# Two of a weight's four column means computed behind the first attention, a new order of the first loads, lone columns by VectorE, last stores by SP

## The chip, the cores and the metric

The kernel runs on one core of one Trainium2 chip. The metric is the device time of one execution in microseconds (us). PE in the profile is TensorE, PEld its weight loads, DVE is VectorE, ACT is ScalarE, POOL is GpSimd, SP is SyncE. "Granted clock" is the share of its full clock that TensorE was given: 1.00 is full, 0.50 is half.

Only one core runs, so there is no second die to compare with. Every ratio below compares runs of two kernels on one chip, interleaved in the same rounds; e9, e12 and e8 before ran on another chip than the other eight experiments.

## The reference

A hash attention (a query sees only the keys whose six sign bits equal its own), then a Fourier mix, a layer norm and a two-layer network:

```python
# q, k, v: (4, 8, 768, 64) f32; proj (64, 6); w_ch1 (512, 2048); w_ch2 (2048, 512)
q_bucket = np.sum((q @ proj > 0) * powers, axis=-1)      # k_bucket the same
scores = np.where(q_bucket == k_bucket, q @ k.T / 8, -1e9)
attn = softmax(scores) @ v                               # sum + 1e-9 below
x = attn as (B, S, H*D) = (4, 768, 512)
u = x + real(fft(fft(x, axis=1), axis=2))
un = (u - mean(u)) / sqrt(var(u) + 1e-6)
out = u + np.maximum(un @ w_ch1, 0) @ w_ch2
```

## The kernel before

The batch is walked in four attentions, each of four head pairs of six key blocks; the mix of one batch is woven between the attention steps of the next. In the first attention there is no mix yet, and there the weight `w1` is prepared: it is turned into the number form that the matmuls use ("narrowing"), and the mean of each column is taken off it, so that the layer norm needs no subtraction. The mean is a matmul with a constant tile. In the kernel before, each of the four column groups of 512 has its mean taken at once when its four slices are narrowed:

```python
def weights(wsb, wdr):
    ...                                   # (cut: buffers, fetches)
    for i, (dst, src) in enumerate(slices):
        if wide:
            narrow(dst, ...)              # 3 VectorE, 3 ScalarE instructions
        fetch(i + depth, nc.gpsimd)
        yield
        if wsb is w1 and i % NDC == NDC - 1:
            f = i // NDC * WC
            ps = pt([P, WC], f"wm{f}")    # a PSUM buffer from a shared pool
            for c in range(NDC):          # NDC = 4
                nc.tensor.matmul(ps, mean, w1[:, c, f : f + WC],
                                 start=(c == 0), stop=(c == NDC - 1))
            for c in range(NDC):
                w = w1[:, c, f : f + WC]
                nc.vector.tensor_tensor(w, w, ps, op=ALU.subtract)
```

The transposes of q and k (`trq`, `trk`) go through the same PSUM pool and are emptied into `qt` and `kt` by VectorE or ScalarE. `fold`, the first part of the mix, has most of its work on VectorE and a small copy of two lone columns on ScalarE, and is started in the last head pair of an attention:

```python
# in attention(b), for each key block c
if c > 1:
    next(half, None)                      # one step of fold(b, 0), last head pair only
...
# in fold
nc.scalar.copy(z[:, :, 2 * n + 1 : 2 * n + 3], f[:, :, 0 : n + 2 : n + 1])
```

The first loads, the bit weights `pw` and the stores follow. The first bits matmuls read `qt` and `pjw`, not `pw`; but the cast of `pw` stands in VectorE's order among the copies that empty `qt`, so they wait for it all the same:

```python
def load(n, others=nc.sync):
    for nm, src in (("q", q), ("k", k), ("v", v)):
        for h in range(2):
            (nc.sync if nm == "q" else others).dma_start(...)
load(0, nc.scalar)                        # q by SP, k and v by ScalarE's queue
...                                       # (cut: proj, off)
nc.sync.dma_start(pwf, cn["pw"].ap())
nc.vector.tensor_copy(pw, pwf)
...
def store(b, T, src):
    nc.gpsimd.dma_start(out[b, ...], src[...])
```

At the very end stands a conditional: a slower general version of the kernel for inputs with very large scores or weights of an unexpected form. With these inputs it is never taken, but every engine has to branch over it.

Of the kernel before, what the change touches and what calls it, by code (L numbers as in the profile page):

```python
# [10 lines left out]
F32 = mybir.dt.float32  # L11
# [5 lines left out]
ALU = mybir.AluOpType  # L17
# [461 lines left out]
def _main(  # L479
# [33 lines left out]
    def pt(shape, name):  # L513

        turn[0] += 1
        if roomy[0] and turn[0] % 2:
            if turn[0] % 4 == 1:
                return ps_o.tile(shape, F32, tag="o", name=name)
            return ps_sc.tile(shape, F32, tag="sc", name=name)
        return ps_1.tile(shape, F32, tag="ps", name=name)  # L520
# [11 lines left out]

    nat = {}

    def load(n, others=nc.sync):
        b, t = divmod(n, NPAIR)
        for nm, src in (("q", q), ("k", k), ("v", v)):
            tag, bufs = ("vn", 2) if nm == "v" else ("qkn", 2)
            tl = wt([P, NT, 2, D], F32, tag, f"{nm}n{n}", bufs)
            for h in range(2):  # L540
                (nc.sync if nm == "q" else others).dma_start(
                    tl[:, :, h, :], src[b, 2 * t + h].rearrange("(p c) d -> p c d", c=NT)
                )
            nat[nm, n] = tl

    warm = const.tile([1, 1], F32, tag="warm", name="warm")
    nc.gpsimd.memset(warm, 0.0)
    load(0, nc.scalar)
    nc.scalar.activation(warm, warm, AF.Exp)

    ident = const.tile([P, P], F32, tag="ident", name="ident")
# [7 lines left out]
        nc.sync.dma_start(pjw[h * D : (h + 1) * D, h * D : h * D + NBITS], proj)  # L559
    off = const.tile([P, 2], F32, tag="off", name="off")  # L560
    nc.sync.dma_start(off, cn["off"].ap())
    pj = const.tile([P, 32], F32, tag="pj", name="pj")
    nc.gpsimd.memset(pj, 0.0)
    for h in range(2):
# [31 lines left out]
    def narrow(dst, raw, low, col):  # L596
# [20 lines left out]
            t, t, AF.Relu, bias=least, scale=-1.0, accum_out=strange[:, col : col + 1]  # L617
        )

    def weights(wsb, wdr):  # L620

        wide = wdr.dtype == I64
        slices = [
            (wsb[:, c, f : f + WC], wdr[c * P : (c + 1) * P, f : f + WC])
            for f in range(0, wdr.shape[1], WC)
            for c in range(wdr.shape[0] // P)
        ]
        raws, masks = [], []
        if wide:
            zt = wt([P, 3, 2 * WC], F32, "z", f"zraw{wdr.shape[0]}", 1)  # L630
            raws += [zt[:, i] for i in range(3)]
            if wsb is w1:
                ft = wt([P, 12, WC], F32, "F", "fraw", 1)
                raws += [
                    ft[:, i : i + 2].rearrange("p i w -> p (i w)") for i in range(0, 8, 2)
                ]
                masks = [ft[:, i] for i in range(8, 12)]

        def fetch(i, queue):
            if i < len(slices):  # L640
                dst, src = slices[i]
                if wide:
                    raw = raws[i % len(raws)].bitcast(I32)
                    queue.dma_start(raw.bitcast(I64), src)
                else:
                    queue.dma_start(dst, src)

        depth = len(raws) or 4
        for i in range(depth):
            fetch(i, nc.sync if wsb is w1 else nc.gpsimd)  # L650
            if wsb is w1 and i == 1:
                load(1)
# [3 lines that stand above are left out]
                mask = masks[i % 4] if masks else wt([P, WC], F32, "u", f"mask{i}", 2)  # L656
                narrow(
                    dst, raws[i % len(raws)].bitcast(I32), mask.bitcast(I32),
                    i if wsb is w1 else len(slices) + i,
                )  # L660
            fetch(i + depth, nc.gpsimd)
            yield
            if wsb is w1 and i % NDC == NDC - 1:

                f = i // NDC * WC
                ps = pt([P, WC], f"wm{f}")
                for c in range(NDC):
                    nc.tensor.matmul(  # L668
                        ps, mean, w1[:, c, f : f + WC],
                        start=(c == 0), stop=(c == NDC - 1),  # L670
                    )
                for c in range(NDC):
                    w = w1[:, c, f : f + WC]
                    nc.vector.tensor_tensor(w, w, ps, op=ALU.subtract)


    xs = {}
# [167 lines left out]
    def attention(b):  # L845
        xs[b] = wt([P, NPAIR, S], F32, "x", f"x{b}")
        pending = []

        def finish():
            n, c, pk, oos, accs = pending.pop(0)  # L850
            values(n, c, pk, oos)
            if c == NT - 1:
                scale(n, oos, accs)

        for t in range(NPAIR):
            n = NPAIR * b + t
            half = fold(b, 0) if t == NPAIR - 1 else iter(())
            if 1 < n + 1 < NPAIR * B:
                load(n + 1)
            ahead = prepare(n + 1) if n + 1 < NPAIR * B else iter(())  # L860
            oos = [ps_o.tile([P, 512], F32, tag="o", name=f"oo{n}_{g}") for g in range(2)]
            accs = [wt([P, 2, HALF], F32, "t3", f"acc{n}_{g}", 4) for g in range(2)]
            first = None
            for c in range(NT):
                new = [weigh(n, g, c) for g in range(2)]
                if c == 0:
                    first = new
                else:
                    for g in range(2):
                        nc.vector.tensor_tensor(  # L870
                            accs[g], first[g][:, :, 0:HALF] if c == 1 else accs[g],
                            new[g][:, :, 0:HALF], op=ALU.add,
                        )
                while pending:
                    finish()
                pending.append((n, c, new, oos, accs))
                if c > 1:
                    next(half, None)
                if c > 0:
                    next(ahead, None)  # L880
                yield
        while pending:
            finish()
# [5 lines left out]
    def store(b, T, src):  # L889

        blk, r = divmod(T * P, HALF)
        at = 0
        while at < P:
            par, i = divmod(r + at, HW)
            w = min(P - at, HW - i)
            s0 = blk * HALF + 2 * i + par
            nc.gpsimd.dma_start(  # L897
                out[b, s0 : s0 + 2 * w - 1 : 2, :], src[at : at + w]
            )
            at += w  # L900
# [8 lines left out]
    def fold(b, cp):  # L909



        x = xs[b]
        if cp == 0:
            zs[b] = wt([P, 2, 2, 2, HALF], F32, "z", f"z{b}", 1)
        for pc in range(2):
            e = wt([P, S], F32, "t3", f"e{b}_{cp}_{pc}", 4)
            nc.vector.tensor_tensor(
                e, x[:, cp], x[:, cp + 2], op=ALU.subtract if pc else ALU.add
            )  # L920
            f = wt([P, 2, HALF], F32, "t3", f"f{b}_{cp}_{pc}", 4)
            for par in range(2):
                nc.vector.tensor_tensor(
                    f[:, par], e[:, 0:HALF], e[:, HALF:S],
                    op=ALU.subtract if par else ALU.add,
                )
            z = zs[b][:, cp, pc]
            n = HALF // 4 - 1
            for at, op in ((0, ALU.add), (2 * n + 3, ALU.subtract)):

                for i, first, last in ((0, 1, n), (n, 2 * n + 2, n + 1)):
                    nc.vector.tensor_tensor(
                        z[:, :, at + i : at + i + last], f[:, :, first : first + last],
                        turned(f, 2 * n + 1 if i == 0 else HALF - 1, last), op=op,
                    )
            nc.scalar.copy(
                z[:, :, 2 * n + 1 : 2 * n + 3], f[:, :, 0 : n + 2 : n + 1]
            )
            yield
# [136 lines left out]
    with tc.manual_schedule(engines={ET.PE, ET.DVE, ET.Activation, ET.Pool}):  # L1076
        for _ in prepare(0):
            pass
        roomy[0] = False
        for i, _ in enumerate(attention(0)):  # L1080
            if i % 5 < 4:
                next(other, None)
        for _ in other:
            pass
    for b in range(B):
        if b > 0:



            wait = 0  # L1090
            if b == 1:
                next(other)
                next(other)
                wait = 2
            steps, done = NPAIR * NT - wait, 2 if b == 1 else 0
            for i, _ in enumerate(attention(b), 1):
                while done * steps < (MIX - LEFT) * (i - wait):
                    next(other)
                    done += 1
# [73 lines left out]
```

## Time and profile before

| what | value |
|---|---|
| time | 1232.55 us median of 6 runs (1231.4 to 1234.67) beside the changed kernel; 1232.8 when the prediction was made |
| TensorE busy | 1187.7 of the 1231.7 us span |
| first matmul / first scores | 7.15 / 14.40 us |
| scale of the first attention's last head pair (VectorE's copy `vs`) | 144.28 us |
| first `trk` transposes behind it | 159.19 us |
| last matmul's end, and from there to the end of the span | 1223.79 us, 7.94 us |

In these tables "scale" is VectorE's copy `vs`, its first step of the division that ends a head pair. The hand-over is the stretch from there to the `trk` transposes of the next attention; `h` is the first layer of the network.

The page's rows by fortieths of the span (30.8 us each; a digit is the busy share in tenths, PEclk the granted clock in tenths) show in one look where there is room:

```profile
PE   7987989999999999999999999999999999999997
DVE  4888759853365547645357464754435653311110
PEclk9999989999999999999999999999999999999999
```

TensorE is short of nine tenths in the first slice, in three slices between 61 and 185 us and in the last. The dip of the clock row to 8 is the slice from 154 to 185 us, behind the wait of 3.53 us before `trk`. VectorE is at seven or eight tenths from 31 to 154 us, where `w1` is prepared.

### The profile page before, as it was taken

The numbers are of one execution on the slowest core, as the hardware profiler recorded it, in microseconds if no ns is written. First come the engines' busy times: TensorE is split into PE (matmuls) and PEld (weight loads), VectorE is DVE, ScalarE is ACT, GpSimd is POOL, SyncE is SP. The second block draws the span as 40 slices with busy tenths as digits, with TensorE's granted clock in tenths as the row PEclk, the third lists the DMA queues.
The fourth block names the chain that finished last, engine by engine and source line by source line (L and its number), as shares of the span: only waits on it lengthen the run. The fifth ranks groups of instructions, "written<-read, shape, count | busy, mean of one in ns | idle before, by whom it ended". The sixth has DMA issues, their size and how long they took to land.

```text
span 1231.7 us, 11839 instructions
## 1 busy us (share of the span) xinstructions
PE 1187.7 (96%) x4585; PEld 592.8 (48%) x4585; DVE 633.8 (51%) x1186; ACT 348.1 (28%) x625; POOL 57.3 (5%) x127
## 2 busy tenths in 40 slices
PE   7987989999999999999999999999999999999997
PEld 4433455444454446444444445544445445754553
DVE  4888759853365547645357464754435653311110
ACT  6876337731222113221223213122112211000000
POOL 1000001101100010000000010000000000001000
PEclk9999989999999999999999999999999999999999
DMA  9421214401010010100101011010000000000000
GB/s 290 127 71 27 47 42 136 153 14 35 18 26 14 22 28 15 24 16 13 43 9 39 1 30 35 1 39 1 22 9 9 1 10 18 1 1 17 9 9 19
DMA packets 82880, 44.24 MB, mean 36 GB/s; under 512 B 76800, under 2 KB 76928, under 8 KB 82816
## 3 DMA queue, kind: packets, MB, share of 16 engines
q1 hardware_dynamic: 74032, 23.22, 7.7%
q0 software_dynamic: 5648, 19.40, 5.0%
q10 hardware_dynamic: 3136, 0.79, 0.4%
q8 instruction: 38, 0.62, 0.2%
q14 instruction: 26, 0.21, 0.1%
HBM read 37.10 MB, written 6.29 MB: 35 GB/s over the span
## 4 chain that ended last, share of the span: by engine, by line
PE 78%; DVE 13%; ACT 4%; issue 2%; DMA 2%; POOL 0%; SPq 0%; POOLq 0%; DVEq 0%; ACTq 0%
PE h L1012 26%; PE o L1040 25%; PE sc L790 9%; PE oo L810 7%; DVE acc L870 3%; DVE pk L799 3%; PE cs L958 2%; ACT pk L796 2%; PE B L987 2%; PE wm L668 1%; PE A L987 1%; PE sum L827 1%; DMA zraw<-in_moe_w_ch_dram 1%; DVE w L607 1%; DVE w L612 1%
## 5 line engine op out<-in xcount | busy, mean ns | idle before, releaser
L1012 PE MATMUL h<-x,w 128*128 128x384 f32 x1024 | 343.5, 491 | 4.8 <-ACT qt L530 2.4
L1040 PE MATMUL o<-w,h 128*128 128x512 f32 x768 | 339.8, 596 | 0.0
L1012 PEld LDWEIGHTS h<-x,w 128*128 128x128 f32 x1024 | 191.0, 190 | 149.3 <-issue 10.4
L799 DVE SCALAR_TENSOR_TENSOR pk<-qb,kb,pk 128x384 f32<-128x384 bf16 x264 | 151.3, 615 | 184.2 <-ACT pk L796 184.0
L1040 PEld LDWEIGHTS o<-w,h 128*128 128x128 f32 x768 | 142.5, 190 | 174.8 <-issue 167.2
L796 ACT ACTIVATE pk<-sc 128x768 f32<-128x768 f32 x192 | 148.8, 809 | 231.3 <-PE sc L790 193.5
L790 PE MATMUL sc<-qt,kt 64*128 64x384 f32 x768 | 191.2, 511 | 0.0
L810 PE MATMUL oo<-pk,vn 128*64 128x385 f32 (+1 forms) x768 | 145.2, 499 | 0.0
L870 DVE TENSOR_TENSOR acc<-acc,pk 128x768 f32<-128x768 f32 x128 | 120.2, 955 | 9.1 <-ACT pk L796 7.5
L790 PEld LDWEIGHTS sc<-qt,kt 64*128 64x128 f32 x768 | 78.4, 188 | 67.4 <-issue 44.3
L1021 ACT ACTIVATE h<-h 128x384 f32<-128x384 f32 x64 | 31.3, 489 | 272.1 <-PE h L1012 272.0
L1019 DVE TENSOR_SCALAR h<-h 128x384 f32<-128x384 f32 x64 | 35.4, 554 | 141.2 <-PE h L1012 141.2
L1046 DVE SCALAR_TENSOR_TENSOR u<-o,rs,u 128x512 f32<-128x512 f32 x24 | 18.0, 751 | 166.7 <-PE o L1040 106.5
L810 PEld LDWEIGHTS oo<-pk,vn 128*64 128x64 f32 x768 | 46.5, 136 | 87.8 <-issue 82.1
L1030 ACT COPY u<-un 128x512 f32<-128x512 f32 x24 | 13.9, 585 | 111.5 <-PE un L1028 111.5
L1036 POOL TENSOR_SCALAR rs<-mv 128x1 f32<-128x1 f32 x24 | 7.7, 321 | 595.5 <-DVE mv L1034 590.6
L897 POOL DMA_DIRECT2D out_dram<-u x32 | 19.4, 607 | 317.1 <-DVE u L1046 255.5
L958 PE MATMUL cs<-ch,z 128*128 128x128 f32 (+3 forms) x192 | 32.1, 321 | 1.2 <-ACT qt L530 1.2
L958 PEld LDWEIGHTS cs<-ch,z 128*128 128x128 f32 x192 | 28.4, 197 | 9.1 <-issue 2.8
L870 DVE TENSOR_TENSOR acc<-pk,pk 128x768 f32<-128x768 f32 x32 | 30.0, 951 | 2.0 <-ACT pk L796 1.7
L965 ACT COPY F<-cs 128x257 f32<-128x257 f32 (+1 forms) x32 | 11.1, 374 | 67.7 <-PE cs L958 67.7
L987 PE MATMUL B<-sq,F 128*128 128x193 f32 (+1 forms) x128 | 26.3, 332 | 1.5 <-DVE bt L747 1.3
(105 smaller groups left out, 799.3 us busy)
## 6 DMA issues: line engine op xcount, KB each, us to landing
zraw<-in_moe_w_ch_dram POOLq DMA_DIRECT2D x21, 512.0 KB, 4.2
qn<-in_q_dram SPq DMA_DIRECT2D x32, 192.0 KB, 3.2
vn<-in_v_dram SPq DMA_DIRECT2D x30, 192.0 KB, 3.2
kn<-in_k_dram SPq DMA_DIRECT2D x30, 192.0 KB, 3.2
out_dram<-u POOLq DMA_DIRECT2D x16, 256.0 KB, 2.4
fraw<-in_moe_w_ch_dram SPq DMA_DIRECT2D x4, 512.0 KB, 7.5
fraw<-in_moe_w_ch_dram POOLq DMA_DIRECT2D x4, 512.0 KB, 4.3
out_dram<-u POOLq DMA_DIRECT2D x16, 128.0 KB, 2.4
```

Source lines behind the costliest of these rows:

```text
L790: nc.tensor.matmul(ps[:, h, 0:HALF], kt[rows, ks], qt[rows, qs], start=kb is not None, stop=True,)
L796: nc.scalar.activation(pk[:, :, 0:HALF], ps[:, :, 0:HALF], AF.Exp, scale=SCALE)
L799: nc.vector.scalar_tensor_tensor(pk[:, h, 0:HALF], qb[:, h, qs], kb[:, h, c : c + 1], pk[:, h, 0:HALF], op0=ALU.is_equal, op1=ALU.mult,)
L810: nc.tensor.matmul(oos[g][h * D : (h + 1) * D, 0:w], nat["v", n][:, c, h, :], pk[g][:, h, 0:w], start=(c == 0), stop=(c == NT - 1),)
L870: nc.vector.tensor_tensor(accs[g], first[g][:, :, 0:HALF] if c == 1 else accs[g], new[g][:, :, 0:HALF], op=ALU.add,)
L897: nc.gpsimd.dma_start(out[b, s0 : s0 + 2 * w - 1 : 2, :], src[at : at + w])
L958: nc.tensor.matmul(ps[:, pc + 2 * lo : pc + 2 * hi - 1 : 2], z[:, cp, pc, par, t * P : (t + 1) * P], ch[:, cp, pc, lo:hi], start=(cp == 0) ...
L987: nc.tensor.matmul(ps[:, cols], F[:, par, k, t, j * P : (j + 1) * P], sq[:, t, k, cols], start=(t == 0), stop=(t == 1),)
L1012: nc.tensor.matmul(ps, w1[:, c, fc * P : (fc + 1) * P], x[:, c, g * HALF : (g + 1) * HALF], start=(c == 0), stop=(c == NDC - 1),)
L1019: nc.vector.tensor_scalar(hr, ps, 0.0, None, op0=ALU.max)
L1021: nc.scalar.activation(hr, ps, AF.Relu)
L1040: nc.tensor.matmul(ps, hs[fc][:, j * P : (j + 1) * P], w2[:, fc, :], start=(fc == 0), stop=(fc == NFC - 1),)
```

## The change

The intent: the third and the fourth mean leave the first attention and are taken together right behind it, kept in two SBUF tiles by ScalarE and subtracted in the hand-over to the second attention. `fold` starts a key block later and its lone columns go to VectorE, so that ScalarE no longer stands behind VectorE's fold. The first loads are asked for in the order q, k, then v: of q and k a half on each of two queues, v on SP's alone. The last batch's stores go by SP instead of GpSimd, so that GpSimd can finish early. The whole diff:

```diff
--- before.py
+++ after.py
@@ -532,20 +532,21 @@
 
     nat = {}
 
-    def load(n, others=nc.sync):
+    def load(n, names="qkv", second=nc.sync):
         b, t = divmod(n, NPAIR)
-        for nm, src in (("q", q), ("k", k), ("v", v)):
+        for nm in names:
+            src = {"q": q, "k": k, "v": v}[nm]
             tag, bufs = ("vn", 2) if nm == "v" else ("qkn", 2)
             tl = wt([P, NT, 2, D], F32, tag, f"{nm}n{n}", bufs)
             for h in range(2):
-                (nc.sync if nm == "q" else others).dma_start(
+                (second if h else nc.sync).dma_start(
                     tl[:, :, h, :], src[b, 2 * t + h].rearrange("(p c) d -> p c d", c=NT)
                 )
             nat[nm, n] = tl
 
+    load(0, "qk", nc.scalar)
     warm = const.tile([1, 1], F32, tag="warm", name="warm")
     nc.gpsimd.memset(warm, 0.0)
-    load(0, nc.scalar)
     nc.scalar.activation(warm, warm, AF.Exp)
 
     ident = const.tile([P, P], F32, tag="ident", name="ident")
@@ -559,6 +560,7 @@
         nc.sync.dma_start(pjw[h * D : (h + 1) * D, h * D : h * D + NBITS], proj)
     off = const.tile([P, 2], F32, tag="off", name="off")
     nc.sync.dma_start(off, cn["off"].ap())
+    load(0, "v")
     pj = const.tile([P, 32], F32, tag="pj", name="pj")
     nc.gpsimd.memset(pj, 0.0)
     for h in range(2):
@@ -616,6 +618,19 @@
         nc.scalar.activation(
             t, t, AF.Relu, bias=least, scale=-1.0, accum_out=strange[:, col : col + 1]
         )
+
+    def average(f):
+        ps = pt([P, WC], f"wm{f}")
+        for c in range(NDC):
+            nc.tensor.matmul(
+                ps, mean, w1[:, c, f : f + WC], start=(c == 0), stop=(c == NDC - 1)
+            )
+        return ps
+
+    def centre(f, avg):
+        for c in range(NDC):
+            w = w1[:, c, f : f + WC]
+            nc.vector.tensor_tensor(w, w, avg, op=ALU.subtract)
 
     def weights(wsb, wdr):
 
@@ -662,16 +677,10 @@
             yield
             if wsb is w1 and i % NDC == NDC - 1:
 
+
                 f = i // NDC * WC
-                ps = pt([P, WC], f"wm{f}")
-                for c in range(NDC):
-                    nc.tensor.matmul(
-                        ps, mean, w1[:, c, f : f + WC],
-                        start=(c == 0), stop=(c == NDC - 1),
-                    )
-                for c in range(NDC):
-                    w = w1[:, c, f : f + WC]
-                    nc.vector.tensor_tensor(w, w, ps, op=ALU.subtract)
+                if f < DFF // 2:
+                    centre(f, average(f))
 
 
     xs = {}
@@ -874,7 +883,7 @@
                 while pending:
                     finish()
                 pending.append((n, c, new, oos, accs))
-                if c > 1:
+                if c > 2:
                     next(half, None)
                 if c > 0:
                     next(ahead, None)
@@ -894,7 +903,7 @@
             par, i = divmod(r + at, HW)
             w = min(P - at, HW - i)
             s0 = blk * HALF + 2 * i + par
-            nc.gpsimd.dma_start(
+            (nc.sync if b == B - 1 else nc.gpsimd).dma_start(
                 out[b, s0 : s0 + 2 * w - 1 : 2, :], src[at : at + w]
             )
             at += w
@@ -933,7 +942,7 @@
                         z[:, :, at + i : at + i + last], f[:, :, first : first + last],
                         turned(f, 2 * n + 1 if i == 0 else HALF - 1, last), op=op,
                     )
-            nc.scalar.copy(
+            nc.vector.tensor_copy(
                 z[:, :, 2 * n + 1 : 2 * n + 3], f[:, :, 0 : n + 2 : n + 1]
             )
             yield
@@ -1082,6 +1091,10 @@
                 next(other, None)
         for _ in other:
             pass
+        means = []
+        for f in range(DFF // 2, DFF, WC):
+            means.append((f, wt([P, WC], F32, "u", f"mean{f}", 2)))
+            nc.scalar.copy(means[-1][1], average(f))
     for b in range(B):
         if b > 0:
 
@@ -1091,6 +1104,8 @@
             if b == 1:
                 next(other)
                 next(other)
+                for f, avg in means:
+                    centre(f, avg)
                 wait = 2
             steps, done = NPAIR * NT - wait, 2 if b == 1 else 0
             for i, _ in enumerate(attention(b), 1):
```

## The prediction

> **What bounds the kernel now.** I read the page first (busy shares, the row of granted clock), then the windows view cut by stage, then the waits of TensorE, then the timelines of TensorE, VectorE and ScalarE around each wait.
>
> ```profile
> span 1231.7 us, 11839 instructions
> PE 1187.7 (96%) x4585; PEld 592.8 (48%) x4585; DVE 633.8 (51%) x1186; ACT 348.1 (28%) x625; POOL 57.3 (5%) x127
> ```
>
> TensorE is busy for 96% of the span, so the change can only win what is left over: 1231.7 - 1187.7 = 44.0 us without a matmul, plus matmuls that ran at a lower clock. The windows view says where (columns: stretch, its length, then busy us of PE, PEld, DVE, ACT, POOL, then granted clock, DMA share, GB/s).
>
> ```profile
> 0.00:7.15 7.15, 0.00 (x1) 0.03 (x1) 0.00 (x0) 1.49 (x2) 1.40 (x18) 1.00 0.85 154
> 77.00:108.50 31.50, 29.16 (x158) 12.74 (x156) 27.39 (x49) 24.14 (x44) 0.00 (x0) 1.00 0.18 41
> 108.50:144.30 35.80, 29.09 (x142) 12.45 (x140) 27.16 (x52) 16.25 (x32) 0.11 (x1) 0.90 0.15 34
> 144.30:160.70 16.40, 11.79 (x75) 5.64 (x72) 15.43 (x35) 7.89 (x15) 0.00 (x0) 0.97 0.21 48
> 205.00:1209.00 1004.00, 994.19 (x3618) 497.41 (x3617) 479.92 (x902) 222.56 (x393) 44.55 (x87) 1.00 0.08 22
> 1209.00:1232.00 23.00, 14.79 (x38) 6.48 (x36) 2.38 (x4) 0.58 (x1) 2.59 (x5) 0.91 0.10 26
> ```
>
> The reader is to see three places with room: 7.15 us before the first matmul, the first attention and its hand-over (to about 161 us), and some 8 us after the last matmul. Between 205 and 1209 only 10 us are idle, and nothing in the change touches most of them. In the first attention VectorE is nearly as busy as TensorE (27.4 of 31.5 us in the third head pair, 15.4 of 16.4 in the hand-over): there it sets the pace when TensorE does not.
>
> The timeline of TensorE shows the two large waits; that of VectorE the mirror image.
>
> ```profile
> 92.64 3.70 PE L668 MATMUL wm<-w,mean 128*128 128x512 f32 x8 [1.08 <-DVE qkb L730]
> 123.39 6.44 PE L668 MATMUL wm<-w,mean 128*128 128x512 f32 x8 [6.24 <-ACT kt L530]
> 159.19 1.13 PE L702 MATMUL trk<-ident,kn 128*128 128x128 f32 x6 [3.53 <-ACT qt L530]
> ```
>
> ```profile
> 96.37 2.48 DVE L674 TENSOR_TENSOR w<-w,wm 128x512 f32<-128x512 f32 x4 [2.67 <-PE wm L668]
> 121.89 1.16 DVE L932 TENSOR_TENSOR z<-f 128x190 f32<-128x190 f32 x4
> 129.87 2.48 DVE L674 TENSOR_TENSOR w<-w,wm 128x512 f32<-128x512 f32 x4 [6.82 <-PE wm L668]
> ```
>
> ```profile
> 121.94 0.20 ACT L936 COPY z<-f 128x4 f32<-128x4 f32 x1 [3.01 <-DVE f L923]
> ```
>
> So the fourth mean waits 6.24 us for a PSUM buffer that ScalarE must empty (kt); ScalarE stands behind a 0.20 us copy of lone columns that itself waits for fold's VectorE work; then VectorE waits 6.82 us for the mean. The eight matmuls of that mean took 6.44 us instead of 3.70.
>
> **What the Trainium skill says.** "TensorE: Matmul & The Clock Gate", Part 1, gives TensorE half its clock after an idle window of about 3.4 us. The trace agrees: its clock records hold two cold stretches of 6.83 us after the start, at 122.1 and at 159.7, right after the waits of 6.24 and 3.53 us. "DMA: Bandwidth & Descriptors", section "Issuing engines are not separate DMA queues", says that a second issuing engine saves only issue time; the order in which bytes are asked for is then what matters. The trace agrees: the first four loads asked for (v, q, k, q) land at 4.05, 4.94, 5.85 and 7.01 whichever queue they are on. The same page, "Latency and other measured facts", puts the first byte of a DMA issued by GpSimd at 1 us and of one by SP at 0.6; no store by SP is in this trace (those by GpSimd land 2.4 us after issue). "Runtime: NRT & Kernel Launch", section "Instruction fetch mechanics", says a taken branch out of the loaded pages waits for a fetch. The end of the trace agrees: VectorE branches at 1224.77 and its next instruction is at 1227.62.
>
> **The change part by part.**
>
> 1. Loading order. q's halves become the first on both queues, so both should land like the first two now: 4.9 us instead of 7.0. k lands like the fourth, near 7.0. That looks like 2 us won, but the order of VectorE's instructions in the changed kernel has: qt copy, cast of pw, qt copy, kt copy. The cast waits for pwf, which now stands on SP behind both halves of v. Today pwf lands at 8.97, the cast runs 9.00 to 9.29, and the bits matmuls start at 9.94 after two qt copies. All of q, k, v (1.18 MB) still precede pwf, at the measured 0.2 MB per us, so I put its landing at 9.1 to 9.4. One copy of 0.34 us less follows the cast: 9.25 + 0.6 = 9.85 against 9.94. So little comes directly; a TensorE that began at 5 us may be at full clock for the bits matmuls (2.93 us for four, cold, against 1.56 warm). I count 0.6 us.
>
> 2. Third mean moved (at 92.64). VectorE goes from the qkb work (done 93.7) straight to the next narrowing, which now starts 98.77: 2.67 us of wait plus 2.40 of centring, 5.1 us less. ScalarE and TensorE can follow: ScalarE is idle from 93.5 to 97.3, and TensorE loses 1.08 + 3.63 us there.
>
> 3. Fourth mean moved, lone columns on VectorE, fold a step later. VectorE's work from 119.8 to 144.3 (24.4 us) loses 6.8 + 0.9 of waits and 2.4 of centring, and gains two copies of about 0.15: 14.6 us. With fold gone from that step it meets acc for key block 3 at once, whose exponentials stand on ScalarE behind a square (1.03 us) and two kt copies (0.84): I find a new wait of 1.8 us. So 24.4 - 14.6 - 1.8 = 8.0 us. The last "acc" of the first attention then ends 5.1 + 8.0 = 13.1 us earlier.
>
> 4. What comes back. Behind that point TensorE has the two means (2 x 3.65 = 7.3 us) and VectorE eight centrings of 0.68 us (about 0.6 start to start) and two lone-column copies, together 5.4 us, all placed by the order ahead of the qt copies that release the trk transposes. VectorE is the bound of this stretch, so trk comes 14.9 + 5.4 + 0.5 = 20.8 us behind the scale of the last head pair instead of 14.9 (159.19 - 144.28). TensorE fills most of it with the means, and I still find about 3.4 us of idle before trk. Net: 13.1 - 5.9 = 7.2 us. The cold stretch at 159.7 cost up to 3.4 us; a wait of 3.4 us may or may not fill a clock window, and after trk TensorE soon waits for a buffer that kt releases, so I count 1.2.
>
> 5. Later batches. Twelve more 0.20 us copies leave ScalarE. TensorE's waits there for ScalarE's qt and kt copies are about 0.6 us each; I count 0.6 in all.
>
> 6. Last stores by SP. Today the last u ends at 1224.64, GpSimd issues at 1224.93, the bytes are down near 1227.4, SP has passed its last semaphore by 1228.4, but GpSimd's drain (4.79 us from 1226.12) holds the end until 1230.9. With GpSimd idle that drain should be over early. SP however has then its branch, and a fetch of about 2.7 us as on VectorE, behind the store: 1225.4 + 2.7, 0.6 for its semaphores, 0.8 for the closing barrier, about 1229.8 against 1231.7. I count 1.6.
>
> Sum: 0.6 + 7.2 + 1.2 + 0.6 + 1.6 = 11.2 us. 1232.8 - 11.2 = 1221.6, said as 1221.5.
>
> **The rivals.** (a) Centring only moves: VectorE, full in the hand-over, gives the win back. For it: 15.4 of 16.4 us busy there, and all eight centrings stand ahead of qt. Against: 6.8 + 2.7 us of its waits vanish, which no moving brings back. If the fold or ScalarE's squares open further waits, the win of steps 3 and 4 falls to about 3 us: 1226. (b) TensorE is the real bound throughout and its waits vanish completely: 1.1 + 6.2 + 2.7 of cold matmuls, 3.5 and 3.4 of the hand-over, about 17 us, with start and tail 1213. Against: VectorE's work in the first attention alone does not allow it. (c) The start wins its full 2 us, because pwf lands early: 1220. (d) SP's branch and hardware queue are no faster than GpSimd's drain: 1223. A slowdown would need a new long wait in the steady part, where no instruction order changes except fold's one step.
>
> **Range and chances.** The main doubt is step 4 (minus 4 to plus 4 us), then the clock's phase and the tail (1.5 each). That gives 1215 to 1227. To be faster by 2% it would have to come under 1208.6, below rival (b); to be slower by 2% it would lose over 24 us. Within 2% is nearly sure.
>
> **What would show it.** Right: no wait of 6 us before a mean, the means back to back behind the sums of the fourth head pair, scale of that pair some 13 us earlier (near 131), trk near 151 with a wait of 2 to 4 us before it, the bits matmuls at 9.3 to 10, VectorE's second qt copy behind the cast of pw, stages from 205 on the same length, and less than 7 us after the last matmul. Wrong: a new wait for ScalarE's kt or for pk in the fourth head pair, a gap over 5 us before trk, a first bits matmul before 9, or an end that still waits for GpSimd's drain.

## The result, and the profile after

| | before | changed |
|---|---|---|
| median of 6 runs, us | 1232.55 (1231.4 to 1234.67) | 1226.78 (1225.33 to 1229.85) |
| profiled span, us | 1231.7 | 1224.7 |
| first matmul / bits / first scores | 7.15 / 9.94 / 14.40 | 5.25 / 9.65 / 14.59 |
| scale of the last head pair | 144.28 | 131.50 |
| its `trk` behind it | 159.19 | 150.41 |
| last matmul's end | 1223.79 | 1214.39 |
| last matmul's end to end of span | 7.94 | 10.36 |

The ratio is 0.9955, with a 95% interval of 0.9941 to 0.997: 0.45% less, within 2%. A ratio here is the mean time of one kernel's runs over that of the other's runs of the same rounds, so it is not quite the ratio of the medians quoted beside it.

Three numbers of the table tell the story. The work of TensorE ends 9.4 us earlier. The span is only 7.0 us shorter, because 2.4 us are lost after the last matmul. And the medians differ by 5.8 us only, mostly because the profiled run of before was slower than its usual one: it took 1233.64 us, 1.1 above the median beside it, where the changed kernel's took 1226.52, 0.3 below its own.

The page of the changed kernel, first the busy shares and then the clock row and TensorE's row:

```profile
span 1224.7 us, 11845 instructions
PE 1184.4 (97%) x4585; PEld 591.8 (48%) x4585; DVE 634.9 (52%) x1202; ACT 346.1 (28%) x611; POOL 52.5 (4%) x119
PE   7999899999999999999999999999999999999996
PEclk9999999999999999999999999999999999999999
```

Of TensorE's three dips one is left (8, from 122 to 153 us), and that of the clock is gone; the last slice has fallen from 7 to 6. TensorE is busy 3.3 us less with the same 4585 matmuls; the next view shows where most of this is.

The groups view of the means (busy us, mean ns of one, then the idle time ahead of them and who ended it), before and then changed:

```profile
L668 PE MATMUL wm<-w,mean 128*128 128x512 f32 x32 | 17.5, 700 | 8.4 <-ACT kt L530 6.2 <-DVE qkb L730 2.1
```

```profile
L625 PE MATMUL wm<-w,mean 128*128 128x512 f32 x32 | 14.5, 602 | 1.1 <-DVE qkb L739 1.1
```

The same 32 matmuls take 3.0 us less, and 7.3 us of waits ahead of them are gone. TensorE's timeline of the changed kernel (start, us, what, and in brackets the wait just before) shows where the moved means went and what came instead:

```profile
130.77 1.74 PE L836 MATMUL sum<-acc,ones 128*64 128x384 f32 x8 [2.39 <-DVE acc L879]
...
132.70 7.13 PE L625 MATMUL wm<-w,mean 128*128 128x512 f32 x16
...
150.41 0.88 PE L711 MATMUL trk<-ident,kn 128*128 128x128 f32 x6 [1.50 <-ACT qt L530]
...
153.66 1.80 PE L967 MATMUL cs<-ch,z 128*128 128x129 f32 x8 [1.37 <-DVE kt L528]
```

The sixteen matmuls of both means stand back to back. The largest waits left are 2.39 us for VectorE's last `acc`, 1.50 before `trk` and 1.37 before `cs`. Before, they were 6.24 and 3.53. In the clock records the two cold stretches of 6.83 us (from 122.1 and 159.7) have become one of 3.41 us (from 154.0).

The windows view of the fourth head pair (from scale to scale) and of the hand-over, as stretch, length, busy us of PE, PEld, DVE, ACT, POOL, then granted clock, DMA share, GB/s. First before, the fourth head pair alone, then changed, both:

```profile
108.98:144.28 35.30, 28.59 (x137) 12.08 (x134) 26.66 (x51) 16.25 (x32) 0.11 (x1) 0.90 0.15 33
```

```profile
104.00:131.50 27.50, 23.00 (x133) 10.16 (x132) 24.40 (x49) 15.86 (x30) 0.11 (x1) 1.00 0.25 57
131.50:150.41 18.91, 17.25 (x81) 7.55 (x79) 18.14 (x42) 5.93 (x10) 0.00 (x0) 1.00 0.10 22
```

The fourth head pair now has the full clock (0.90 before) and takes 27.5 us instead of 35.3, with VectorE busy for 24.4 of them, TensorE for 23.0. In the hand-over VectorE is busy for 18.1 of 18.9 us: there it sets the pace. The long steady part has hardly moved: from the first matmul of `h` to the end of the last matmul it took 1018.5 us, against 1019.1 before (204.68 to 1223.79 and 195.89 to 1214.39).

At the start, VectorE and TensorE of the changed kernel:

```profile
6.16 0.42 DVE L528 COPY qt<-trq 128x192 f32<-128x192 f32 x1 [6.16 <-PE trq L711]
8.98 0.29 DVE L571 CAST pw<-pwf 128x256 bf16<-128x256 f32 x1 [2.41 <-DMA pwf<-k_pw]
9.19 0.40 DVE L528 COPY qt<-trq 128x192 f32<-128x192 f32 x1
```

```profile
7.09 1.51 PE L711 MATMUL trk<-ident,kn 128*128 128x128 f32 x6 [0.33 <-DMA kn<-in_k_dram]
9.65 2.93 PE L737 MATMUL bitsq<-qt,pjw 128*128 128x384 f32 x4 [1.05 <-DVE qt L528]
12.38 2.29 PE L737 MATMUL bitsk<-kt,pjw 128*128 128x384 f32 x4
```

For comparison, the same two places in the kernel before:

```profile
9.00 0.29 DVE L569 CAST pw<-pwf 128x256 bf16<-128x256 f32 x1 [9.00 <-DMA pwf<-k_pw]
```

```profile
9.94 2.93 PE L728 MATMUL bitsq<-qt,pjw 128*128 128x384 f32 x4
12.66 1.57 PE L728 MATMUL bitsk<-kt,pjw 128*128 128x384 f32 x4
```

TensorE begins 1.9 us earlier, and the bits matmuls only 0.3 us earlier: VectorE's cast of `pw` stands between its two `qt` copies and waits for a load that lands at the same time as before. The `bitsk` matmuls then took 2.29 us in place of 1.57, since full clock came at 14.04 in this run and at 12.89 before.

At the end, the timeline before and changed:

```profile
1223.89 0.75 DVE L1046 SCALAR_TENSOR_TENSOR u<-o,rs,u 128x512 f32<-128x512 f32 x1 [12.26 <-PEq L1137]
1224.93 0.65 POOL L897 DMA_DIRECT2D out_dram<-u  x1 [12.07 <-DVEq L1137]
```

```profile
1214.48 0.75 DVE L1055 SCALAR_TENSOR_TENSOR u<-o,rs,u 128x512 f32<-128x512 f32 x1 [12.26 <-PEq L1152]
1215.26 0.34 SPq L906 DMA_DIRECT2D out_dram<-u  x1
```

From the last `u` on there is no work left in either kernel, only the store and the closing. What the engines' sequencers did then is not in the page. It is taken from the raw records of each trace, in us from the start of the span. "Landed" is when the semaphores of a store show all its bytes written; a drain is the instruction with which an engine closes:

| step | before (GpSimd stores) | changed (SP stores) |
|---|---|---|
| last store issued | 1224.93, by GpSimd | 1215.26, by SP |
| issuer's last branch over the fallback | 1225.66 | waits for the landing first |
| store landed, as SP sees it | 1227.88 | 1218.39 |
| SP's last branch | long past (1015.09) | 1218.52 |
| SP's next instruction | | 1221.28 |
| a second gap among SP's closing waits | none | 1221.80 to 1223.59 |
| GpSimd's closing drain | 1226.12 to 1230.91 | over long before (1203.76, 4.13 us) |
| SP's drain | 1228.43 | 1223.93 |
| end of span | 1231.74 | 1224.74 |

Each engine branches twice at the conditional. SP's first branch came right behind the store (1215.65) and cost nothing; then it passed the semaphores of its queue's transfers one by one, stood at that of the last store, and branched again. The fetch stands behind this second branch.

So the changed kernel did free itself of GpSimd's drain, as meant. But SP now has in series: 3.1 us to the landing, 2.8 behind its branch, 0.5 of waits, a second gap of 1.8, then 0.3 and the closing barrier of 0.8. The records of transfers name instruction fetches: two packets of 8 KB lie behind the branch (from 1219.43) and one in the second gap (1222.12 to 1222.42), though not which engine they were for.

### The profile page after: what moved, and what is told of

The parts are those of the page before. It is cut to its first block, busy times and chain, and to the rows that moved or that the text cites. A ratio compares the mean times of both kernels' runs of the same rounds, so it can differ in the third digit from the quotient of the medians. Undisturbed runs are those within 1.5% of the kernel's fastest.

```text
span 1224.7 us, 11845 instructions
## 1 busy us (share of the span) xinstructions
PE 1184.4 (97%) x4585; PEld 591.8 (48%) x4585; DVE 634.9 (52%) x1202; ACT 346.1 (28%) x611; POOL 52.5 (4%) x119
## 5 line engine op out<-in xcount | busy, mean ns | idle before, releaser
L1030 ACT ACTIVATE h<-h 128x384 f32<-128x384 f32 x64 | 31.3, 489 | 277.3 <-PE h L1021 277.1
L831 ACT ACTIVATE x<-oo,vs 128x384 f32<-128x384 f32 x32 | 16.8, 577 | 41.8 <-DVE vs L828 41.8
L996 PE MATMUL A<-sq,F 128*128 128x193 f32 (+1 forms) x128 | 26.3, 334 | 1.5 <-DVE x L1012 1.5
```

The source lines that it names most:

```text
L996: nc.tensor.matmul(ps[:, cols], F[:, par, k, t, j * P : (j + 1) * P], sq[:, t, k, cols], start=(t == 0), stop=(t == 1),)
L1030: nc.scalar.activation(hr, ps, AF.Relu)
```

## The experiments

Eleven runs, in four groups. "Before" beside them was 1233.6 to 1233.8 us (9 to 12 runs, 1231.3 to 1236.3). In short:

| run | what | median us (range, runs) | ratio to before (95%) |
|---|---|---|---|
| the change | all four parts | 1226.78 (1225.33 to 1229.85, 6) | 0.9955 (0.9941 to 0.997) |
| e1 | the change, stores by GpSimd | 1224.77 (1222.43 to 1227.8, 6) | 0.9933 (0.992 to 0.9946) |
| e2 | before, only stores by SP | 1234.61 (1234.1 to 1236.12, 5) | 1.0011 (0.9999 to 1.0024) |
| e3 | the change, very last store by ScalarE | 1228.0 (1225.49 to 1233.33, 6) | 0.9953 (0.9941 to 0.9965) |
| e4 | the change, `pw` cast by GpSimd | 1225.49 (1224.39 to 1226.46, 5) | 0.9938 (0.9925 to 0.9951) |
| e5 | before, only the moved means | 1223.66 (1222.79 to 1223.79, 4) | 0.992 (0.9905 to 0.9934) |
| e6 | before, only columns and fold's step | 1233.42 (1231.57 to 1234.14, 4) | 0.9999 (0.9984 to 1.0013) |
| e8 after | the change without the fallback | 1222.42 (1218.44 to 1224.72, 4) | 0.9904 (0.9886 to 0.9923) |
| e8 before | before without the fallback | 1232.31 (1230.98 to 1233.74, 5) | 0.999 (0.9977 to 1.0004) |
| e9 | the change, loading undone | 1226.99 (1225.47 to 1227.86, 5) | 0.994 (0.9926 to 0.9953) |
| e10 | e1 and e4 together | 1223.52 (1222.41 to 1227.06, 6) | 0.9926 (0.9913 to 0.9939) |
| e12 | e10, columns and fold's step undone | 1222.53 (1221.83 to 1223.36, 4) | 0.9907 (0.9892 to 0.9922) |

The changed kernel itself was timed at another time than the experiments, beside a before of 1232.55; where one of them is set against it, medians and ratios can differ by about 1 us, and less than that is not read as a difference.

All outputs are right. The two without the fallback are only probes: they would be wrong for the inputs that need it.

### The tail: who issues the last stores

Theory A: SP's stores put its wait for the landing, its branch and the fetch in series, and this costs about 2 us against GpSimd's drain. The rival: the tail is noise of one trace, or follows from other parts of the change.

**e1, the change with all stores by GpSimd.**

```diff
-            (nc.sync if b == B - 1 else nc.gpsimd).dma_start(
+            nc.gpsimd.dma_start(
```

> The changed kernel with the last batch's stores back on GpSimd; all else as changed. Theory A (on SP the landing of the last store and the fetch behind SP's branch stand one after the other, on GpSimd they overlap): the stretch from the last matmul's end to the end of the span goes from 10.4 back to about 8.0 us, the last matmul stays where it is (1214.3), and the time is about 2.4 us below the changed kernel's median of 1226.8, near 1224.4. Rival B (the tail is better on SP, and the missing gain was lost elsewhere or is spread between executions): the time rises by 1.6 us to about 1228.4, with a tail of 12 us.

From last matmul to end it took 7.95 us (10.36 in the changed kernel), and the time fell by 2.0 us to 1224.77 (2.7 by the ratios). So the loss belongs to the stores; that it is the series of waits is for the next runs to show.

**e2, the kernel before with only the stores of the last batch by SP.** The edit is the same line the other way.

> The kernel before with nothing changed but the last batch's stores, which go to SP. Theory A: the tail grows from 7.9 to about 10.4 us and the kernel is slower than before by 2.4 us, near 1235.0. Rival B: it is faster than before by 1.6 us, near 1231.

The last part took 9.89 us instead of 7.94, as theory A has it for this part alone. The median is 0.8 us over before where 2.4 were expected, and the interval of the ratio just reaches 1: the tail shows the cost, the time alone would not. SP's waits view of this run, and then that of the changed kernel, hold the same line (waited for: us in total, times, longest):

```profile
SPq L1137 <- SPq L1137: 2.3, 1, 2.3
```

```profile
SPq L1152 <- SPq L1152: 2.3, 1, 2.3
```

SP waits 2.3 us for a semaphore of its own store, and does so ahead of its branch: L1137 and L1152 are the lines of the conditional in the two kernels. The raw records of e2 then show the branch at 1228.58, the next instruction at 1231.14 and the second gap from 1231.75 to 1233.32.

**e3, the change with only the very last tile stored by ScalarE**, so that SP's branch comes early.

```diff
-            (nc.sync if b == B - 1 else nc.gpsimd).dma_start(
+            (nc.gpsimd if b < B - 1 else nc.scalar if T == NT - 1 else nc.sync).dma_start(
```

> The changed kernel with the very last tile's store issued by ScalarE, the five others of the last batch by SP. Theory A: SP has its branch behind it while the last store is under way, ScalarE waits for its landing (about 4 us after the last matmul) and then for one fetch of 2.7 us, the closing barrier takes 0.8: tail about 7.5 us, time near 1224.0. Rival C (it is the store from a hardware queue itself that is slow, whichever engine issues it): tail still 10 us or more, time as the changed kernel's 1226.8.

A miss for theory A: the last part took 10.42 us, as its rival C had it (but not for C's reason, as the next run shows). SP waits ahead of its branch for ScalarE's store too (until 1225.05, branch at 1225.19, next instruction at 1228.36), so another issuer on a hardware queue does not take the landing out of the series. The profiled run was also the slowest of the six: besides the one around 155, which lasted 10.24 us here, it has cold stretches of 3.41 us at 131.3 and 240.5, and its span is 7.9 us longer than that of the fastest run of the same kernel.

**e8 after, the changed kernel without the conditional.**

```diff
-    with tc.If(large > 0, preferred_fallthrough_block=False):
-        _any_scores(tc, *args, cn)
```

> The changed kernel without the conditional fallback behind it (right for this data, which never takes it; no kernel to keep), so no engine branches at the end. Theory A: SP goes from the landing of the last store (some 4.0 us after the last matmul) straight to its semaphores, so the tail shrinks from 10.4 to about 5.7 us and the time from 1226.8 to about 1222.2. Rival C (the store from SP's queue is slow in itself): tail stays above 8 us.

The last part took 3.90 us, even less than expected: SP's store at 1218.53 was seen landed at 1220.56, 2.0 us later, and the end followed 1.0 us behind. Neither the fetch nor the second gap is there. That the second gap is a second fetch is likely: it goes with the branch in three traces (changed, e2, e3), in each an instruction packet of 8 KB falls there (from 1222.12, 1231.72 and 1229.06), and here no instruction is fetched at the end. The time fell by 4.4 us by the medians, less than the 6.5 of the tail; in the profiled run, which has four cold stretches, the last matmul ended at 1217.66, 3.3 us later than in the changed kernel.

**e8 before, the same cut in the kernel before.** It was run on another chip.

> The kernel before without the conditional fallback (never taken with these inputs), stores on GpSimd as before. Theory A2 (in the kernel before GpSimd's drain of 4.8 us behind the last store sets the end, and no branch stands in that chain): the drain still follows the last issue, last matmul's end to end of the span 7.0 to 7.9 us, time 1232 to 1233.6, at most 1 us won, where the changed kernel won 6.5 us in its tail by the same cut. Rival (the branch and its fetch delay the end here too, through some engine's last instructions): tail 4 to 5.5 us, time 1230 to 1231.

The last part took 7.35 us instead of 7.94. GpSimd's drain (1222.88 to 1228.28, 5.4 us) sets the end with the branch or without it. So the same cut is worth 6.5 us of tail behind SP's stores and 0.6 behind GpSimd's (1.5 by the medians, with an interval that holds 1), and the branch is the cause of SP's long tail.

### The start: what the bits matmuls wait for

**e4, the change with the cast of `pw` by GpSimd.**

```diff
-    nc.vector.tensor_copy(pw, pwf)
+    nc.gpsimd.tensor_copy(pw, pwf)
```

> The changed kernel with the cast of pw done by GpSimd instead of VectorE. Theory D (at the start the second qt copy only waits for the cast of pw that stands ahead of it on VectorE): the bits matmuls start near 7.7 us instead of 9.65, the first scores near 12.6 instead of 14.6, and the last matmul ends about 1.9 us earlier; time near 1224.9. Rival E (the first attention is paced by ScalarE and by the loads of w1, an earlier start is swallowed by 40 us): the first mean's matmuls still start near 37.9 and the time is unchanged.

TensorE and VectorE at the start of this run:

```profile
7.07 1.51 PE L711 MATMUL trk<-ident,kn 128*128 128x128 f32 x6 [0.34 <-DMA kn<-in_k_dram]
8.38 2.76 PE L737 MATMUL bitsq<-qt,pjw 128*128 128x384 f32 x4
10.94 1.81 PE L737 MATMUL bitsk<-kt,pjw 128*128 128x384 f32 x4
```

```profile
6.77 0.41 DVE L528 COPY qt<-trq 128x192 f32<-128x192 f32 x1 [0.22 <-PE trq L711]
```

The second `qt` copy no longer waits for the cast, the bits matmuls follow `trk` without a gap at 8.38 instead of 9.65, and the first scores come at 12.82 instead of 14.59. The bits come at 8.38 and not at the 7.7 expected, because `trk` itself begins only when k has landed. The median falls by 1.3 us of the 1.9 expected; the ratios give 2.1, and the last matmul of the profiled run ends 2.2 us earlier (1212.22).

**e9, the change with the loading order of the kernel before.** It was run on another chip. The edit takes back the lines of loading in the diff of the change.

> The changed kernel with the loading order of the kernel before, all else as changed. Theory D (the new order wins nothing by itself, because the bits matmuls wait for pw, whose cast on VectorE waits for pwf): first matmul back at 7.15 us, bits at 9.9, first scores near 14.4, and a time within 0.5 us of the changed kernel, about 1226.5. Rival (an earlier first matmul and an earlier warm clock are worth the 2 us): about 1228.8, first scores 2 us later than in the changed kernel.

1226.99 against 1226.78 us by the medians, 0.994 against 0.9955 by the ratios: the new order alone wins nothing that these runs can see. (The theory words it wrongly: the bits matmuls wait for `qt`, whose second copy stands behind the cast of `pw`.) First matmul 7.11, bits 9.92, first scores 13.92, so in this run even earlier than with the new order (14.59), because full clock came at 11.69. With the very start of the changed kernel, e1 had it at 12.86 and the first scores at 14.13: the moment of full clock moves by over 1 us between runs of one start.

### The middle: the means, the columns and fold's step

**e5, the kernel before with only the moved means** (the functions `average` and `centre`, the block of two means behind the first attention, and the centring in the second; nothing else of the diff).

```diff
-                ps = pt([P, WC], f"wm{f}")
-                ...                              # matmuls and subtractions at once
+                if f < DFF // 2:
+                    centre(f, average(f))
...
+        means = []
+        for f in range(DFF // 2, DFF, WC):
+            means.append((f, wt([P, WC], F32, "u", f"mean{f}", 2)))
+            nc.scalar.copy(means[-1][1], average(f))
...
+                for f, avg in means:
+                    centre(f, avg)
```

> The kernel before with only the two means moved behind the first attention (loads, lone columns, fold's step and stores as before). Theory F (the moved means alone free VectorE and TensorE; the lone columns on ScalarE hold up nothing once no mean waits behind kt): the scale of the fourth head pair starts near 131 as in the changed kernel (131.5, before 144.3), the last matmul ends about 9 us earlier (near 1215), tail 7.9, time near 1223.9. Rival G (ScalarE's copy behind fold still delays kt and the exponentials): a TensorE wait of 3 us or more in the fourth head pair, the scale near 135 and the time near 1228.

1223.66 us: this part alone gains 10 us, more than the whole change. The scale of the last head pair is at 131.11 (131.50 changed), the last matmul ends at 1213.91 (1214.39 changed). The wait that the columns and fold's step were to remove is still there, on ScalarE and then on TensorE:

```profile
116.17 0.20 ACT L942 COPY z<-f 128x4 f32<-128x4 f32 x1 [3.01 <-DVE f L929]
```

```profile
117.62 1.56 PE L734 MATMUL bitsq<-qt,pjw 128*128 128x384 f32 x4 [1.98 <-ACT kt L530]
...
132.44 7.13 PE L623 MATMUL wm<-w,mean 128*128 128x512 f32 x16
```

but the sixteen matmuls of the means begin at 132.44 us, no later than in the changed kernel (132.70), where these waits are gone. From scale to scale the fourth head pair took 27.90 us here and 27.50 in the changed kernel, so with no mean behind it the wait costs little, about 0.4 us.

**e6, the kernel before with only the lone columns on VectorE and fold a step later.**

```diff
-                if c > 1:
+                if c > 2:
...
-            nc.scalar.copy(
+            nc.vector.tensor_copy(
```

> The kernel before with only the lone columns on VectorE and fold one step later (all four means where they were). Theory F: the fourth mean still waits for kt, but only behind ScalarE's square, so 3 us instead of 6.2 and no cold stretch at 122 us; the last matmul ends some 5 us earlier and the time is near 1227.5. Rival: VectorE's work for fold, now later, is met by the scale and nothing is won: 1232.

A miss: 1233.42 against 1233.6, nothing won. TensorE's waits in this run:

```profile
119.73 5.40 PE L668 MATMUL wm<-w,mean 128*128 128x512 f32 x8 [2.99 <-ACT kt L530]
...
156.54 1.54 PE L702 MATMUL trk<-ident,kn 128*128 128x128 f32 x6 [4.59 <-ACT qt L530]
```

The wait before the fourth mean halves, from 6.24 to 2.99, and the scale of the last head pair comes 2.4 us earlier (141.86). The wait before `trk` grows from 3.53 to 4.59, but 2.65 us are still won there (156.54 against 159.19). They are lost behind it: the first matmul of the first layer (`h`) is at 204.59 against 204.68. In between the profiled run has a cold stretch of 13.65 us from 155.3, where before had one of 6.83; that this is the cause fits, and was not tested.

### Putting together what helps

**e10, the change with the stores of e1 and the cast of e4.**

> The changed kernel with two repairs: the last batch's stores on GpSimd again and the cast of pw on GpSimd. If both gains are separate (2.0 us at the end, 1.3 us at the start by the medians of their own runs) the time is near 1223.5, below both kernels, with a tail of 7.9 us and the first scores near 12.8 us.

1223.52 us, as expected.

**e12, the same without the columns and fold's step**, which leaves of the change the means and the loading, and adds the cast by GpSimd.

> The kernel before with the two means moved, the new loading order and the cast of pw on GpSimd; lone columns stay with ScalarE, fold keeps its step, the last stores stay with GpSimd. Theory (means and start add up, columns and fold's step are worth nothing once the means are moved): bits at 8.4 us, first scores at 12.2, scale of the fourth head pair near 129.4, last matmul's end near 1212.2, tail 7.95, time about 1222.0, that is 1.5 us below the run with means, columns and start (1223.5) and 1.5 below the means alone (1223.7). Rival (with the start earlier the columns on VectorE are worth something, since ScalarE's copy again waits 3 us for fold in the fourth head pair): 1224 to 1225, with a wait of over 2 us of TensorE for a buffer that ScalarE empties between 115 and 131 us.

1222.53 us, the fastest complete version: 0.9907 of before, where the changed kernel had 0.9955. The columns and fold's step are worth nothing beside the moved means, or cost about 1 us. The intervals of e10 and e12 overlap, and the two ran on different chips, so their sign is not settled; e1 and e5, on one chip, differ by 1.1 us in the same direction and overlap too. The rival's sign, a wait of over 2 us for a buffer that ScalarE empties, is there (2.04 us), but not its time of 1224 to 1225. TensorE's longest waits of this run and of e10 stand in different places. First e12, then e10:

```profile
116.38 1.56 PE L737 MATMUL bitsq<-qt,pjw 128*128 128x384 f32 x4 [2.04 <-ACT kt L530]
122.99 1.74 PE L737 MATMUL bitsk<-kt,pjw 128*128 128x384 f32 x4 [1.89 <-DVE qkb L739]
```

```profile
127.92 2.13 PE L836 MATMUL sum<-acc,ones 128*64 128x384 f32 x8 [2.17 <-DVE acc L879]
149.16 0.88 PE L711 MATMUL trk<-ident,kn 128*128 128x128 f32 x6 [1.51 <-ACT qt L530]
```

e12 waits early in the head pair and not at its end; e10 waits at its end, in front of the means, and had cold stretches of 3.41 us at 129.1 and 153.0 there where e12 had none. At the first `h` e12 is 1.9 us ahead (192.73 against 194.58). But the profiled runs end almost level (last matmul at 1213.10 and 1213.33), because e12 has its cold stretch later, at 232.1. So the traces do not show where the 1 us of the medians comes from.

## Why the prediction was right or wrong

The class (within 2%) was right, and 1226.78 lies inside the range of 1215 to 1227, at its very edge. The gain was not: 5.8 us by the medians (5.5 by the ratio), about half of the 11.2 predicted. The terms of the sum, one by one; measured is the profiled run of the changed kernel against that of before:

| term, as the prediction put it | predicted | measured |
|---|---|---|
| 1 loading order | +0.6 | -0.2 (first scores 14.40 to 14.59) |
| 2 and 3: the last head pair's scale, start included | +13.7 | +12.8 (144.28 to 131.50) |
| 1 to 4: `trk` behind it | +7.8 | +8.8 (159.19 to 150.41) |
| 1 to 4 and the clock: first `h` | +9.0 | +8.8 (204.68 to 195.89), so 0.0 for the clock's 1.2 |
| 1 to 5: last matmul's end | +9.6 | +9.4 (1223.79 to 1214.39) |
| 6 last stores by SP | +1.6 | -2.4 (7.94 to 10.36) |

**Step 6 is the step that failed**, with the wrong sign: 4.0 us of the 4.2 us that the span lacks to the sum. The prediction put the fetch of SP's branch right behind the issue of the store and beside the landing: "1225.4 + 2.7, 0.6 for its semaphores, 0.8 for the closing barrier". (These make 1229.5, not the "about 1229.8" that it gives, and neither is 1.6 us below 1231.7.) The runs showed that SP waits for the landing before the branch that is followed by the fetch (2.3 us in the waits view), and that there is a second gap of 1.8 us behind the fetch. These are the two terms that were missing, and they are in series. e1 gave 2.0 us back by undoing this part alone, e2 showed the same tail of 9.9 us in the kernel before, and e8 took the branch out and had a tail of 3.9 us. The trace of before held the clue, though only in its raw records: between its two branches SP passed eight semaphores one by one (1014.53 to 1015.04), GpSimd a single one. All eight were free at that moment, so no view showed a wait, and the prediction took the cheaper case. Its other half was right: with no store behind it GpSimd's drain was over early (1203.76 to 1207.90).

**Step 1** had the mechanism right, but its 0.6 us did not come. The cast waits for `pwf`, which landed at 8.96, a little before the 9.1 to 9.4 estimated, and the bits matmuls began at 9.65 (9.85 predicted). The rest, a warm clock for the bits, did not come: `bitsq` took the same 2.93 us. e9 saw nothing won by the whole part, and e4 shows that it is the cast that hides it.

**Steps 2 and 3** held, in size too: from scale to scale the third head pair went from 31.3 to 26.2 us (5.2 less, 5.1 predicted) and the fourth from 35.3 to 27.5 (7.8 less, 8.0 predicted). The waits of 6.24 us and of VectorE's 6.82 are gone, the means stand back to back behind the sums, the scale is at 131.50 ("near 131") and `trk` at 150.41 ("near 151"). In step 4 the hand-over was priced a little high: `trk` came 18.9 us behind the scale, not 20.8, and waited 1.50 us, not 3.4. What the prediction could not tell is that step 3's second and third part (columns, fold) add nearly nothing to the moved means: it summed them with the fourth mean. e5 has 7.4 of the 7.8 us without them. A wait of `acc` for `pk` in the fourth head pair, named as a sign of being wrong but also priced at 1.8 us in step 3, came with 1.16 us at the longest. **Step 5** stays open: the steady part came out 0.6 us shorter, as said, but it lies anywhere from 1018.2 to 1020.4 us in the traces of the other runs, with the columns moved or not.

**The clock** did not give its 1.2 us. Two cold stretches of 6.83 us became one of 3.41, but from `trk` to the first `h` both traces took 45.5 us. In e5 and e12, with no cold stretch there, it took 43.7 and 43.8. (The prediction has the first stretch "right after" the wait of 6.24 us; it began at 122.12, inside that wait, which ended at 123.39.) So that the sum was within 0.2 us at the first `h` and at the last matmul is in part luck: the scale fell 0.9 short, the hand-over was priced 1.9 too high, and the clock's 1.2 was missing. The clock also makes single runs differ. The six spans of the changed kernel range over 4.5 us, those of e3 over 7.9, and the longer ones have in the main the lower mean granted clock.

Of the rivals, (a) did not come: the hand-over kept the win. Nor did (b), with its 1213. Rival (d), that SP's branch and queue are no faster than GpSimd's drain, was the right doubt, but it put them level (1223), and they were worse. Rival (c), a start that wins 2 us, is what e4 and e12 make true in part by moving one cast.

## What to carry to other kernels

When work is taken from an engine's tail, write down for the new engine the whole series to its last instruction: issue, landing, what it waits for before a branch, fetch, closing waits; an engine that was idle at the end in the old trace shows none of these waits. When a change has several parts, run each alone: here one part (the moved means) was worth 10 us, one nothing, one nothing by itself until a cast was moved, and one cost 2 us. And look at who stands behind a wait: one of 2 us on TensorE cost about 0.4 us where no mean followed (e5), while behind the one of 6.2 us before the fourth mean VectorE in turn waited 6.8.

## What the Trainium skill lacked or had wrong

- "Runtime: NRT & Kernel Launch", section "Instruction fetch mechanics", says that a taken branch out of the loaded pages waits for a fetch, and gives no time. Here 2.6 to 3.2 us lay between SP's branch and its next instruction (changed 1218.52 to 1221.28, e2 1228.58 to 1231.14, e3 1225.19 to 1228.36), and about 1.6 to 1.8 us more in a second gap behind it. Without the branch both were gone. Instruction packets of 8 KB lie in both gaps.
- No page says which engine waits for the last stores of a kernel, and when: SP passed the semaphores of its own and of ScalarE's stores before its last branch (2.3 us of wait in the changed kernel and in e2), while GpSimd branched at once behind its store (1225.66) and left the wait for it to SP.
- "GPSIMD Engine Reference" has no time for GpSimd's closing drain. It took 4.1 to 5.4 us, with the last store just issued (4.79 in before) as well as where SP issues the last stores (4.13 in the changed kernel).
- "DMA: Bandwidth & Descriptors", section "Latency and other measured facts", has first bytes of 0.6 us for a DMA issued by SP and 1 us by GpSimd. The order agrees: the first packet of this kernel's last store of 256 KB came 0.84 us after SP's issue (changed, e8 after) and 1.22 after GpSimd's (before, e8 before). What the page does not have is the time to the semaphore beside a branch: without the branch 2.0 us from SP's issue and 2.4 from GpSimd's, with it 3.1 and 2.9. In the changed kernel 14 of the store's 16 completions had come within 2.0 us, and two came at 1217.98 and 1218.37; instruction packets were moved at the same time (8 KB at 1217.02), and none in e8. That they held up the two fits, but no run isolates it.
- "TensorE: Matmul & The Clock Gate", Part 1, says that the clock window is free-running and that its phase varies from run to run. The runs agree: in one start, that of the change and e1, full clock came at 14.04 and 12.86 us, and cold stretches came in multiples of 3.41 us. It puts the penalty of the ramp below 1% of a typical span. That holds here (7.9 us of 1224 between two runs of e3, at 0.990 and 0.996 of the clock), but what it leaves unsaid is that this is larger than the 5.8 us that this change gained, so a single profile can't measure such a change.
